# K and Q transposed by DMA from batch 2 on, and a rearranged start, in a fused local-attention and feed-forward kernel

## The chip, the cores and the metric

The kernel runs on one core of one Trainium2 chip. The metric is the time of one execution on the device in microseconds (us). Engines: TensorE (PE; its weight loads are listed as PEld), VectorE (DVE), ScalarE (ACT), GpSimd (POOL) and SyncE (SP). Each works through its own queue of instructions in order. SP and POOL also issue DMAs.

## What is computed

Eight batches of eight heads, 576 positions, head size 64. Attention is local (32 positions to each side) plus eight global positions, which see and are seen by all. Its output, 4608 rows of 512, goes through a feed-forward of 2048.

```python
scores = scale * np.matmul(q, k.transpose(0, 1, 3, 2))
mask = np.abs(pos[:, None] - pos[None, :]) <= window
mask = mask | is_global[:, None] | is_global[None, :]
scores = np.where(mask, scores, -1000000000.0)
attn = softmax(scores)                      # over the keys
x = np.matmul(attn, v)                      # to rows (batch, position) x (head, d)
h = x @ w_in
g = s * np.maximum(h, 0.0) ** 2 + b
out = g @ w_out
```

## The kernel before

**Pairs.** The 64 (batch, head) problems are taken two heads at a time: 32 pairs, four per batch. A pair has five chunks of 120 keys; the first eight of a chunk's 128 rows hold the global keys. For each chunk c, `qk` (L425) computes the scores of both heads into PSUM (tile pss, two buffers, pool ps_s), ScalarE takes the exponential (tile e), and VectorE multiplies by the mask (tile em). `pv` (L444) multiplies all five em with V (vring) and with ones (the sums), into po (one buffer). `norm_steps` (L462) are ln (s1) and exp(-ln) (s2, tile rep) on ScalarE, and the product with po into xt on VectorE; it also adds the global queries' parts up (gs), and after the fourth pair of a batch makes xg from them, which `scatter` (L498) copies into the global columns of xt on POOL, eight copies.

**K and Q.** The scores need K and Q with the head size on partitions. `load_kq` (L140) has POOL load them, cast to bf16, in a packed form (six consecutive rows on a partition, tile six, a ring of NR = 6 pairs). `trans` (L384) transposes them on TensorE, 24 small transposes per pair, into a PSUM tile pst. `trans_a` (K) and `trans_b` (Q) queue the copies out of PSUM: K by VectorE into kt (L403), Q by VectorE for one head and ScalarE for the other into qbd (L416), block-diagonal. `put_kq` (L373) adds the global columns. V is loaded as it is (`load_v`, L148, tile natv, four pairs), cast into vring (`cast_v`), and `put_v` (L366) writes the global rows.

**Globals.** For every two batches `gather` (L224) fetches the global rows of K, Q and V by indirect DMA, and the five steps of `globals_of` (L327) cast, transpose and place them; round_v and move do so for V, with 16 small matmuls each into psv and a copy to gvx (L361).

**Feed-forward.** `moe_quanta` (L508) yields 288 quanta: nine tiles of 512 rows, each with 16 psh quanta (first matrix, L523; a Relu to r on ScalarE, L530, and the square to g on VectorE, L533) and 16 pso quanta (second matrix, L538; every fourth ends with a store). `Q(n)` runs the next n, if the counter quanta allows. Sums of w_out's rows (wsum, L705) make the bias row in pairs 8 to 15; eight early output tiles are held back until it is there, and then released.

**Order.** The order on every engine is the one in which the code is written. A pair has eight slots (`run_pair`, L583): slots 0 to 4 one score chunk each, slot 6 the next pair's transposes, this pair's pv and put_v; in each slot come first its own matmuls, then extra work (ex), then the work queued in the slot before (list `later`, run as prev), then the slot's quanta. Hence the copies out of PSUM, queued in slot 6, run in slot 7. `first_pair` (L614) is the form for pairs 0 to 3, which have no feed-forward beside them: five slots, and at its end a flush of all that is queued. Between it and the loop (L669 to L697) stand pair 3's pv, pair 4's transposes, loads, scatter(0) and the weight loads. In the loop (L720), pair p first issues `load_kq(p + 4)` on POOL and `load_v(p + 3)` on SP.

Of the kernel before, what the change touches and what calls it, by code (L numbers as in the profile page):

```python
# [16 lines left out]
P = 128  # L17
B, H, S, D = 8, 8, 576, 64
NG = 8
# [16 lines left out]
NR = 6  # L36
NV = 4
NJ = 6
NP6 = S // NJ
N6 = NCH * KC // NJ  # L40
# [23 lines left out]
def kernel(  # L64
# [27 lines left out]
    stage = ctx.enter_context(tc.tile_pool(name="stage", bufs=3))  # L92
# [33 lines left out]
    six = {t: const.tile([P, NR, 2, NJ, D], BF16, name=f"six{t}", tag=f"six{t}") for t in "kq"}  # L126
    natv = const.tile([P, NV, NCH, 2, D], FP32)
# [19 lines left out]

    def load_v(eng, p):  # L148
        bi, hp = divmod(p, 4)
        for hh in range(2):  # L150
            o = v[bi, 2 * hp + hh, 0, 0].offset

            last = p == NPAIR - 1 and hh == 1
            for c, nch, n in ((0, NCH - 1, KC), (NCH - 1, 1, S - KC * (NCH - 1))) if last else (
                (0, NCH, KC),
            ):
                eng.dma_start(
                    out=natv[NG : NG + n, p % NV, c : c + nch, hh],
                    in_=bass.AP(
                        tensor=v.tensor, offset=o + c * KC * D,  # L160
                        ap=[[D, n], [KC * D, nch], [1, D]],
                    ),
                )
# [12 lines left out]
    clear(qbufs[0][0:D, 1], LQ)  # L176
    clear(qbufs[0][D:P, 0], LQ)
    clear(natv[0:NG].rearrange("p n c h d -> p (n c h d)"), NV * NCH * 2 * D)
    for t in "kq":
        nc.vector.memset(six[t][NP6:P, :, :, NJ - 1], 0.0)  # L180
    for t in gqd:
        nc.vector.memset(t[0:D, 1], 0.0)
        nc.vector.memset(t[D:P, 0], 0.0)
# [40 lines left out]
    def gather(bb):  # L224

        gfs[bb] = globp.tile([P, 3, D], FP32, tag="gf", name="gf")
        for i, t in enumerate("kqv"):
# [23 lines left out]
    load_kq(1)  # L251
    nc.vector.memset(kidx[0:NG], 100000.0)
# [34 lines left out]
    def build_masks():  # L287
        for c in range(NCH):
# [13 lines left out]
    for j in range(2):  # L302
        nc.gpsimd.dma_start(
            out=win_t[:, :, 1024 * j : 1024 * j + 1024],
            in_=w_in2[:, :, 1024 * j : 1024 * j + 1024],
        )
    greg_p = [
# [19 lines left out]
    def globals_of(bb):  # L327
# [3 lines left out]
        gvx[bb] = globp.tile([NG, 8, 2, D], BF16, tag="gvx", name="gvx")  # L331
# [22 lines left out]
        def move(i):  # L354
            ps = ps_m.tile([P, 4, 2, D], FP32, tag="moe", name="psv")
            for hp in range(4):
                for hh in range(2):
                    r0 = D * hh + 32 * i + NG * hp
                    nc.tensor.matmul(ps[:NG, hp, hh], ident[:, r0 : r0 + NG], gb[:, 2])
            later.append(  # L360
                lambda: nc.vector.tensor_copy(out=gvx[bb][:, 4 * i : 4 * i + 4], in_=ps[:NG])  # L361
            )

        return round_kq, turn, round_v, lambda: move(0), lambda: move(1)

    def put_v(eng, p):  # L366
        bb, x = divmod(p, 8)
        eng(  # L368
            out=vring[0:NG, p % NV].rearrange("g c h d -> g c (h d)"),
            in_=view(gvx[bb][:, x], [0, NCH], [1, 2 * D]),  # L370
        )

    def put_kq(p):  # L373
        bb, x = divmod(p, 8)
        nc.vector.tensor_copy(
            out=view(ktile[p][:], [P, NCH], [1, NG]),
            in_=view(gkt[bb][:, NG * x : NG * x + NG], [0, NCH], [1, NG]),
        )
# [19 lines left out]
    def trans_a(p):  # L398
        ps = trans("k", p)
        kt = ktp.tile([P, LQ], BF16, tag="kt", name="kt")  # L400
        ktile[p] = kt
# [7 lines left out]
    def trans_b(p):  # L409
# [173 lines left out]
    def run_pair(p, nq, extra):  # L583
# [3 lines left out]
        if hp == 0:  # L587
            open_batch(bi)
        for s in range(8):
# [7 lines left out]
            elif s == 5:  # L597
                if hp == 0 and bi > 1:
                    later.append(lambda: scatter(bi - 1))
            elif s == 6:  # L600
                if more:
                    trans_a(p + 1)
                    trans_b(p + 1)
                pv(p)
                pending.extend(norm_steps(p))
            if s == 6 and more:
                put_v(V if p < 7 else G, p + 1)
# [39 lines left out]
    flush()  # L647
    warm(3)
# [45 lines left out]
    load_v(nc.gpsimd, 7)  # L694
    onesf = const.tile([P, P], FP32)
# [95 lines left out]
```

## Time and profile before

| | |
|---|---|
| median of 9 runs | 397.71 us (395.76 to 397.77) |
| the profiled execution | 398.78 us |
| its span, in which the profile counts | 397.0 us |
| mean granted TensorE clock | 0.952 |
| first feed-forward matmul (psh) | 49.96 us |
| pair 8 begins | 87.35 us |
| last pair ends | about 328 us |

The page of the profile gives busy time by engine, then the span in 40 slices: each digit is the busy share in tenths, and PEclk is the TensorE clock that was granted, in tenths of full speed. A group of instructions is named by line, engine, operation and output<-input. "A <- B" in a list of waits means that A's engine stood idle until B ended. The chain of waits follows the execution back from its last instruction, at each step to what released it. Busy time of one instruction is from its start to its end; neighbours on an engine overlap, so their starts can lie closer together than their durations.

### The profile page before, as it was taken

To read this page: it belongs to the slowest core of one execution; us is meant where nothing else is said; L and a number is where in the kernel's file an instruction comes from. 1 tells how busy PE (TensorE), PEld (TensorE's weight loads), DVE (VectorE), ACT (ScalarE), POOL (GpSimd) and SP (SyncE) were. 2 spreads that over 40 slices of the span, in tenths; PEclk is the share of its full clock that TensorE was granted. 3 is DMA by queue.
4 is the path that set the end of the run, shared out by engine and by line. 5 is a ranking of instruction groups with operands and counts; after the bars stand their busy time and mean duration, and the time that the engine had idled before them with its cause. 6 is when DMAs were issued, how large, how long until landed. Compare 5 with 4: busy or idle time off the path is not lost.

```text
span 397.0 us, 9076 instructions
## 1 busy us (share of the span) xinstructions
PE 357.9 (90%) x3533; PEld 209.9 (53%) x3533; DVE 262.2 (66%) x648; ACT 216.2 (54%) x416; POOL 128.5 (32%) x224
## 2 busy tenths in 40 slices
PE   6766398899899979899989998999999999999996
PEld 2343244455555556456755775567656654554442
DVE  5764557677987798778877777687667763432431
ACT  5665558744684467446764676357745761630710
POOL 7753186145760560229600900383004001000000
PEclk8775579999999999999999999999999999999999
DMA  5999389835981290059534840575021002001002
GB/s 96 185 209 201 67 149 187 170 57 99 225 155 50 29 202 2 26 128 186 128 99 125 165 74 2 115 151 87 2 85 54 2 0 82 29 22 64 21 26 79
DMA packets 56558, 38.07 MB, mean 96 GB/s; under 512 B 34792, under 2 KB 49128, under 8 KB 56516
## 3 DMA queue, kind: packets, MB, share of 16 engines
q0 software_dynamic: 18784, 20.07, 30.0%
q1 hardware_dynamic: 37732, 17.43, 17.3%
q8 instruction: 27, 0.44, 0.5%
q14 instruction: 15, 0.12, 0.1%
HBM read 41.68 MB, written 9.44 MB: 129 GB/s over the span
## 4 chain that ended last, share of the span: by engine, by line
PE 63%; DVE 18%; ACT 13%; issue 3%; DMA 2%; ACTq 0%; DVEq 0%; POOLq 0%
PE pso L538 30%; PE psh L523 17%; PE po L453 6%; PE pss L427 5%; ACT r L530 4%; DVE g L533 4%; DVE em L434 3%; PE pst L392 3%; ACT qbd L416 3%; DVE xt L490 3%; ACT e L431 2%; DVE qbd L416 2%; DVE kt L403 2%; DVE wsum L705 2%; DMA sixk<-in_k_dram 2%
## 5 line engine op out<-in xcount | busy, mean ns | idle before, releaser
L523 PE MATMUL psh<-xt,win_t 128*128 128x512 bf16 (+7 forms) x1024 | 141.7, 289 | 0.0
L538 PE MATMUL pso<-wout_t,g 128*128 128x512 bf16 x576 | 137.1, 379 | 1.8 <-DVE gvx L361 1.8
L530 ACT ACTIVATE r<-psh 128x512 bf16<-128x512 f32 x144 | 87.9, 627 | 66.6 <-PE psh L523 64.1
L523 PEld LDWEIGHTS <-win_t 128*128 128x128 bf16 x1024 | 85.6, 98 | 48.8 <-issue 6.1
L431 ACT ACTIVATE e<-pss 128x384 bf16<-128x384 f32 (+1 forms) x160 | 76.5, 483 | 36.5 <-PE pss L427 32.1
L533 DVE TENSOR_TENSOR g<-r 128x512 bf16<-128x512 bf16 x144 | 64.0, 448 | 43.7 <-ACT r L530 41.4
L538 PEld LDWEIGHTS <-g 128*128 128x128 bf16 x576 | 54.5, 98 | 65.3 <-issue 5.1
L434 DVE TENSOR_TENSOR em<-e,mask 128x384 bf16<-128x384 bf16 (+1 forms) x160 | 62.3, 392 | 21.3 <-ACT e L431 20.8
L427 PE MATMUL pss<-qbd,kt 128*128 128x384 bf16 (+1 forms) x160 | 51.3, 330 | 20.8 <-ACT qbd L416 16.7
L501 POOL COPY xt<-xg 128x4 bf16 x64 | 14.4, 225 | 124.5 <-DVE xt L490 120.9
L416 ACT COPY qbd<-pst 64x600 bf16<-64x600 bf16 x32 | 20.9, 653 | 54.5 <-DVE qbd L416 54.3
L552 DVE SCALAR_TENSOR_TENSOR osb<-pso,s_bc,bias_row 128x512 f32<-128x512 f32 x28 | 20.9, 747 | 37.4 <-PE pso L538 37.4
L368 POOL COPY vring<-gvx 8x640 bf16<-8x640 bf16 x24 | 18.4, 769 | 55.3 <-DVE gvx L361 54.0
L427 PEld LDWEIGHTS <-kt 128*128 128x128 bf16 x160 | 15.4, 99 | 30.2 <-DVE qbd L379 11.2
L490 DVE TENSOR_TENSOR xt<-po,rep 128x600 bf16<-128x600 f32 x32 | 24.9, 779 | 4.7 <-ACT rep L488 4.3
L453 PE MATMUL po<-em,vring 128*64 128x160 bf16 (+3 forms) x448 | 21.8, 231 | 6.7 <-DVE xt L490 6.4
L403 DVE COPY kt<-pst 128x600 bf16<-128x600 bf16 x32 | 24.8, 774 | 4.1 <-PE pst L392 4.1
L484 ACT ACTIVATE ln<-po 128x640 f32<-128x640 f32 x32 | 22.6, 706 | 5.1 <-PE po L453 5.1
L416 DVE COPY qbd<-pst 64x600 bf16<-64x600 bf16 x32 | 24.5, 765 | 0.7 <-PE pst L392 0.7
L488 ACT ACTIVATE rep<-ln 128x640 f32<-128x640 f32 x32 | 24.3, 759 | 0.1
L453 PEld LDWEIGHTS <-vring 128*64 128x64 bf16 x448 | 18.3, 117 | 9.9 <-DVE xt L490 5.8
L143 POOL DMA_DIRECT2D sixk<-in_k_dram x32 | 21.3, 664 | 6.8 <-issue 5.9
(81 smaller groups left out, 269.5 us busy)
## 6 DMA issues: line engine op xcount, KB each, us to landing
natv<-in_v_dram SPq DMA_DIRECT2D x51, 150.0 KB, 3.9
out_dram<-osb SPq DMA_DIRECT2D x28, 256.0 KB, 2.1
sixk<-in_k_dram POOLq DMA_DIRECT2D x32, 144.0 KB
sixq<-in_q_dram POOLq DMA_DIRECT2D x32, 144.0 KB
wst<-in_moe_w_out_dram POOLq DMA_DIRECT2D x8, 512.0 KB
win_t<-in_moe_w_in_dram POOLq DMA_DIRECT2D x2, 1024.0 KB
wout_t<-in_moe_w_out_dram POOLq DMA_DIRECT2D x4, 512.0 KB
out_dram<-osbh SPq DMA_DIRECT2D x8, 256.0 KB
```

What stands on the lines that cost most here:

```text
L403: lambda: nc.vector.tensor_copy(out=view(kt[:, NG:], [P, NCH], [NJ, KC // NJ], [1, NJ]), in_=view(ps[:], [KC // NJ, NCH], [1, KC // NJ], [ ...
L416: eng(out=view(qbufs[p % 3][r, hh], [P, NCH], [HB + NG, 2], [NJ, n], [1, NJ]), in_=view(ps[r], [2 * n, NCH], [n, 2], [1, n], [NP6, NJ]),)
L427: nc.tensor.matmul(ps[:], ktile[p][:, P * c : P * c + P], qbufs[p % 3][:, :, LO[c] : HI[c]])
L431: nc.scalar.activation(e[:], ps[:], AF.Exp, scale=SCALE)
L434: later.append(lambda: nc.vector.tensor_mul(em[:], e[:], masks[c]))
L453: nc.tensor.matmul(po[D * hh : D * hh + D, a : a + n], onesb[:] if part else vring[:, p % NV, c, hh], emt[(p, c)][:, hh, x : x + n], start ...
L488: nc.scalar.activation(rep[:], ln[:], AF.Exp, scale=-1.0)
L490: lambda: nc.vector.tensor_tensor(out=xt[:, hp].rearrange("p (c a j) -> p c a j", c=NCH, a=2), in0=halves(po[:, 0:LQ]), in1=halves(rep[:]) ...
L523: nc.tensor.matmul(psh[:, d0 : d0 + n], win_t[:, a, f * P : f * P + P], xts[bi][:, a, x0 : x0 + n], start=(a == 0 and j == 0), stop=(a == ...
L530: nc.scalar.activation(r[:], psh[:], AF.Relu)
L533: later.append(lambda g=g, r=r: nc.vector.tensor_mul(g[:], r[:], r[:]))
L538: nc.tensor.matmul(pso[:], gl[f][:, u * P : u * P + P], wout_t[:, f], start=(f == 0), stop=(f == 15),)
```

## The change

Three things. **From batch 2 on (pairs 8 to 31)** K and Q are loaded in their natural layout, in fp32, by SP (`load_nat`, with V), four pairs ahead. ScalarE casts them into natb (`round_nat`) in slots 5 and 7 of pair p-2. One transposing DMA of SP (`turn_nat`), 128 x 1280 elements of bf16 between SBUF tensors, follows in slot 7. In slot 5 of pair p-1 `place_nat` uses K where it landed, copies Q's halves into qbd with two VectorE copies, and calls put_kq. The global rows of V for batches 2 to 7 come by eight POOL loads into gvall, so the gathers fetch only K and Q there, and put_v stays on VectorE. **In the first pairs** the copies out of PSUM go into the slot of their transposes (list now), put_v and cast_v stand in other slots, the flush at the end is gone, V's global steps of batch 0 come after pair 0, and the masks are built in two parts. **Pair 4** runs its score slots as a fifth first pair, and only its slots 5 to 7 in run_pair, with 0, 1 and 2 quanta where all its slots had 6. Pairs 8 to 31 have one quantum per slot as before, so the three fall to the end. All weight loads, gvall and gather(1) stand ahead of scatter(0) in POOL's order.

```diff
-NR = 6
+NR = 5
 NV = 4
+NSIX = 8
+KT0 = 16
+QT0 = KT0 + NCH * P
...
+    nat = {t: const.tile([P, NV, NCH, 2, D], FP32, name=f"nat{t}", tag=f"nat{t}") for t in "kq"}
+    natb = [const.tile([P, 2, NCH * P], BF16, name=f"natb{i}", tag=f"natb{i}") for i in range(2)]
...
+    def load_nat(eng, t, p):
+        bi, hp = divmod(p, 4)
+        dst = natv if t == "v" else nat[t]
+        parts = ((0, 0, HB), (HB, HB, HB)) if t == "q" else ((NG if t == "v" else 0, 0, KC),)
+        for hh in range(2):
+            o = src[t][bi, 2 * hp + hh, 0, 0].offset
+            for r, a, n in parts:
+                runs = [(0, NCH, n)]
+                if p == NPAIR - 1 and hh == 1:
+                    runs = [(0, NCH - 1, n), (NCH - 1, 1, min(n, S - KC * (NCH - 1) - a))]
+                for c, nch, m in runs:
+                    eng.dma_start(
+                        out=dst[r : r + m, p % NV, c : c + nch, hh],
+                        in_=bass.AP(
+                            tensor=src[t].tensor, offset=o + (c * KC + a) * D,
+                            ap=[[D, m], [KC * D, nch], [1, D]],
+                        ),
+                    )
     def load_v(eng, p):
-        bi, hp = divmod(p, 4)
+        load_nat(eng, "v", p)
+    kqt = {}
+    def round_nat(i, t, p):
+        nc.scalar.copy(
+            out=natb[p % 2][0:KC, i].rearrange("p (c h d) -> p c h d", c=NCH, h=2),
+            in_=nat[t][0:KC, p % NV],
+        )
+    def turn_nat(p):
+        kqt[p] = kqp.tile([P, QT0 + NCH * P], BF16, tag="kqt", name="kqt")
+        nc.sync.dma_start_transpose(
+            out=kqt[p][:, KT0:].rearrange("p (c x) -> p c x", x=P),
+            in_=natb[p % 2][:].rearrange("p t x -> p (t x)"),
+        )
+    def place_nat(p):
+        ktile[p] = kqt[p][:, KT0 - NG : KT0 - NG + LQ]
         for hh in range(2):
-            o = v[bi, 2 * hp + hh, 0, 0].offset
-            last = p == NPAIR - 1 and hh == 1
-            for c, nch, n in ((0, NCH - 1, KC), (NCH - 1, 1, S - KC * (NCH - 1))) if last else (
-                (0, NCH, KC),
-            ):
-                eng.dma_start(
-                    out=natv[NG : NG + n, p % NV, c : c + nch, hh],
-                    in_=bass.AP(
-                        tensor=v.tensor, offset=o + c * KC * D,
-                        ap=[[D, n], [KC * D, nch], [1, D]],
-                    ),
-                )
+            r = slice(D * hh, D * hh + D)
+            nc.vector.tensor_copy(
+                out=view(qbufs[p % 3][r, hh], [P, NCH], [HB + NG, 2], [1, HB]),
+                in_=view(kqt[p][r, QT0:], [P, NCH], [HB, 2], [1, HB]),
+            )
+        put_kq(p)
...
-    def gather(bb):
+    def gather(bb, ts="kq"):
...
     gather(0)
     load_kq(1)
+    gather(0, "v")
...
             in_=w_in2[:, :, 1024 * j : 1024 * j + 1024],
         )
+        if j == 0:
+            load_kq(4)
...
+        if bb:
+            return round_kq, turn
         return round_kq, turn, round_v, lambda: move(0), lambda: move(1)
...
-        bb, x = divmod(p, 8)
+        g = gvx[0][:, 2 * D * p :] if p < 8 else gvall[:, 2 * D * (p - 8) :]
         eng(
             out=vring[0:NG, p % NV].rearrange("g c h d -> g c (h d)"),
-            in_=view(gvx[bb][:, x], [0, NCH], [1, 2 * D]),
...
-    def trans_a(p):
+    def trans_a(p, later=later):
...
-    def trans_b(p):
+    def trans_b(p, later=later):
...
-        if hp == 0:
+        if hp == 0 and p > 4:
             open_batch(bi)
-        for s in range(8):
+        for s in range(8) if p > 4 else range(NCH, 8):
             prev, later[:] = list(later), []
             if s < NCH:
                 qk(p, s)
                 if s == 2 and more:
                     cast_v(A if p < 7 else G, p + 1)
             elif s == 5:
-                if hp == 0 and bi > 1:
+                if hp == 0:
                     later.append(lambda: scatter(bi - 1))
+                if p == 4:
+                    cast_v(A, 5)
             elif s == 6:
-                if more:
+                if p + 1 < NSIX:
                     trans_a(p + 1)
                     trans_b(p + 1)
                 pv(p)
                 pending.extend(norm_steps(p))
             if s == 6 and more:
-                put_v(V if p < 7 else G, p + 1)
+                put_v(V, p + 1)
             for f in extra.get(s, ()):
                 f()
             for f in prev:
     def first_pair(p):
-        if p == 0:
-            open_batch(0)
+        if p % 4 == 0:
+            open_batch(p // 4)
         for s in range(NCH):
             prev, later[:] = list(later), []
+            now = []
             qk(p, s)
             if s in (1, 2):
-                if p < 3:
-                    (trans_a, trans_b)[s - 1](p + 1)
+                if p < 4:
+                    (trans_a, trans_b)[s - 1](p + 1, now)
                 if p:
                     pv(p - 1, (s - 1,))
                     if s == 2:
                         pending.extend(norm_steps(p - 1))
             elif s > 2:
                 step()
-                if s == 3 and p < 3:
+                if s == 4 and p < 4:
                     cast_v(A, p + 1)
-            for f in prev:
+            for f in prev + now:
                 f()
-            if s == 4 and p < 3:
-                put_v(V, p + 1)
-        flush()
+            if s == 3 and p:
+                put_v(V, p)
...
     warm(12)
     trans_a(0)
     flush()
+    build_masks((0, 1))
     warm(3)
     trans_b(0)
     warm(8)
     flush()
     steps0 = globals_of(0)
-    build_masks()
     steps0[0]()
     steps0[1]()
-    warm(4)
+    warm(2)
     flush()
     put_kq(0)
+    build_masks((2, 3, 4))
     cast_v(A, 0)
-    for t in qbufs[1:]:
-        clear(t[0:D, 1], LQ)
-        clear(t[D:P, 0], LQ)
+    first_pair(0)
     for f in steps0[2:]:
         f()
     flush()
     put_v(V, 0)
-    for p in range(4):
+    load_v(nc.gpsimd, 4)
+    load_kq(5)
+    for p in (1, 2, 3, 4):
         first_pair(p)
-    pv(3)
-    pending.extend(norm_steps(3))
+        if p == 1:
+            load_v(nc.gpsimd, 5)
     for i in (1, 2, 3):
         rows_of(i)
-    for p in (4, 5):
-        load_kq(p)
-        load_v(nc.gpsimd, p)
     load_w_out(0)
     load_w_out(1)
     load_kq(6)
-    step()
-    trans_a(4)
-    flush()
-    step()
-    cast_v(A, 4)
-    trans_b(4)
-    flush()
-    put_v(V, 4)
-    scatter(0)
     nc.sync.dma_start(out=s_bc[:], in_=_bcast_dram(moe_s[:], P))
     nc.sync.dma_start(out=b_bc[:], in_=_bcast_dram(moe_b[:], P))
     load_v(nc.gpsimd, 6)
...
     load_w_out(3)
     load_kq(7)
     load_v(nc.gpsimd, 7)
+    gvall = const.tile([NG, (B - 2) * H * D], BF16)
+    for i in range(NG):
+        nc.gpsimd.dma_start(
+            out=gvall[i : i + 1].rearrange("o (b h d) -> o b h d", b=B - 2, h=H),
+            in_=v[2:, :, ds(greg_p[i], 1), :].rearrange("b h o d -> o b h d"),
+        )
     onesf = const.tile([P, P], FP32)
     nc.vector.memset(onesf[:], 1.0)
     quanta[0] = 32
...
         bi, hp = divmod(p, 4)
         nq = [1] * 8
         if bi == 1:
-            nq = [0, 1, 1, 1, 0, 1, 1, 1] if hp else [0, 0, 1, 1, 1, 1, 1, 1]
+            nq = [0, 1, 1, 1, 0, 1, 1, 1] if hp else [0, 0, 0, 0, 0, 0, 1, 2]
         elif hp == 0:
             quanta[0] += 32
         if p + 4 < NPAIR:
-            load_kq(p + 4)
-        if p >= 5 and p + 3 < NPAIR:
-            load_v(nc.sync, p + 3)
+            for t in "kqv":
+                load_nat(nc.sync, t, p + 4)
         if p % 8 == 4 and p + 4 < NPAIR:
             gather((p + 4) // 8)
         ex = {}
-        if p % 8 == 7 and p + 1 < NPAIR:
-            for s, f in enumerate(globals_of((p + 1) // 8)):
-                ex.setdefault(s, []).append(f)
+        def at(s, f, *a):
+            ex.setdefault(s, []).append(lambda: f(*a))
+        if p >= 6 and p + 2 < NPAIR:
+            at(5, round_nat, 0, "k", p + 2)
+            at(7, round_nat, 1, "q", p + 2)
+            at(7, turn_nat, p + 2)
+        if p % 8 > 4 and p + 3 < NPAIR:
+            if p % 8 == 5:
+                steps = globals_of((p + 4) // 8)
+                at(7, steps[0])
+            elif p % 8 == 6:
+                at(1, steps[1])
+        if p >= 7 and p + 1 < NPAIR:
+            at(5, place_nat, p + 1)
         if 8 <= p < 15:
             for s in (4, 7):
                 if adds:
-                    ex.setdefault(s, []).append(adds.pop(0))
+                    at(s, adds.pop(0))
         if 7 <= p < 15:
             adds.extend(wpiece(p - 7))
         if p == 15:
-            ex.setdefault(2, []).append(lambda: [f() for f in adds] and adds.clear())
-            ex[2].append(bias)
+            for f in adds:
+                at(2, f)
+            at(2, bias)
         if p > 15 and held_rows:
-            ex.setdefault(4, []).append(release)
-            ex.setdefault(7, []).append(release)
+            at(4, release)
         run_pair(p, nq, ex)
     flush()
     while pending:
```

More of the change, by code (lines that the diff above doesn't have):

```diff
@@ L91 @@
     mop = ctx.enter_context(tc.tile_pool(name="mop", bufs=3))
-    stage = ctx.enter_context(tc.tile_pool(name="stage", bufs=3))
+    stage = ctx.enter_context(tc.tile_pool(name="stage", bufs=2))
+    kqp = ctx.enter_context(tc.tile_pool(name="kqp", bufs=2))
     globp = ctx.enter_context(tc.tile_pool(name="globp", bufs=2))
@@ L174, in clear @@
         nc.scalar.copy(out=ap, in_=view(zero[0 : ap.shape[0]], [0, n]))
-    clear(qbufs[0][0:D, 1], LQ)
-    clear(qbufs[0][D:P, 0], LQ)
+    for t in qbufs[:2]:
+        clear(t[0:D, 1], LQ)
+        clear(t[D:P, 0], LQ)
     clear(natv[0:NG].rearrange("p n c h d -> p (n c h d)"), NV * NCH * 2 * D)
+    clear(qbufs[2][0:D, 1], LQ)
+    clear(qbufs[2][D:P, 0], LQ)
     for t in "kq":
         nc.vector.memset(six[t][NP6:P, :, :, NJ - 1], 0.0)
+    for t in natb:
+        nc.vector.memset(t[96:P], 0.0)
     for t in gqd:
@@ L222 @@
     gfs = {}
-    def gather(bb):
-        gfs[bb] = globp.tile([P, 3, D], FP32, tag="gf", name="gf")
-        for i, t in enumerate("kqv"):
+    def gather(bb, ts="kq"):
+        if bb not in gfs:
+            gfs[bb] = globp.tile([P, 3, D], FP32, tag="gf", name="gf")
+        for t in ts:
+            i = "kqv".index(t)
             nc.gpsimd.indirect_dma_start(
@@ L285, with build_masks @@
     masks = []
-    def build_masks():
-        for c in range(NCH):
+    def build_masks(cs):
+        for c in cs:
             m = const.tile([P, W[c]], BF16, name=f"mask{c}", tag=f"mask{c}")
@@ L330, in globals_of @@
         gkt[bb] = globp.tile([P, D], BF16, tag="gkt", name="gkt")
-        gvx[bb] = globp.tile([NG, 8, 2, D], BF16, tag="gvx", name="gvx")
+        if bb == 0:
+            gvx[0] = const.tile([NG, 16 * D], BF16, name="gvx", tag="gvx")
         def round_kq():
@@ L360, in move @@
             later.append(
-                lambda: nc.vector.tensor_copy(out=gvx[bb][:, 4 * i : 4 * i + 4], in_=ps[:NG])
-            )
+                lambda: nc.vector.tensor_copy(
+                    out=gvx[bb][:, 512 * i : 512 * i + 512],
+                    in_=ps[:NG].rearrange("g a h d -> g (a h d)"),
+                )
+            )
+        if bb:
+            return round_kq, turn
         return round_kq, turn, round_v, lambda: move(0), lambda: move(1)
     def put_v(eng, p):
-        bb, x = divmod(p, 8)
+        g = gvx[0][:, 2 * D * p :] if p < 8 else gvall[:, 2 * D * (p - 8) :]
         eng(
             out=vring[0:NG, p % NV].rearrange("g c h d -> g c (h d)"),
-            in_=view(gvx[bb][:, x], [0, NCH], [1, 2 * D]),
+            in_=view(g, [0, NCH], [1, 2 * D]),
         )
@@ L375, in put_kq @@
         nc.vector.tensor_copy(
-            out=view(ktile[p][:], [P, NCH], [1, NG]),
+            out=view(ktile[p], [P, NCH], [1, NG]),
             in_=view(gkt[bb][:, NG * x : NG * x + NG], [0, NCH], [1, NG]),
@@ L396, in trans @@
         return ps
-    def trans_a(p):
+    def trans_a(p, later=later):
         ps = trans("k", p)
         kt = ktp.tile([P, LQ], BF16, tag="kt", name="kt")
-        ktile[p] = kt
+        ktile[p] = kt[:]
         later.append(
@@ L694 @@
     load_v(nc.gpsimd, 7)
+    gvall = const.tile([NG, (B - 2) * H * D], BF16)
[3 more added lines that the diff above has]
+            in_=v[2:, :, ds(greg_p[i], 1), :].rearrange("b h o d -> o b h d"),
+        )
     onesf = const.tile([P, P], FP32)
```

## The prediction, made before the changed kernel ran

> **What bounds the kernel now.** I read the page first (busy shares, slices), then TensorE's waits by stage, the chain of waits, then single pairs in the timeline.
>
> ```profile
> PE 357.9 (90%) x3533; PEld 209.9 (53%) x3533; DVE 262.2 (66%) x648; ACT 216.2 (54%) x416; POOL 128.5 (32%) x224
> ...
> PE   6766398899899979899989998999999999999996
> ...
> PEclk8775579999999999999999999999999999999999
> ```
>
> TensorE is the busiest engine, and full from about the eighth slice (80 us) on, at the whole granted clock. Before that it has holes, and its clock falls (0.50 from 30 to 55 us). I cut the span in three: a head up to 87.35 us (pairs 0 to 7), the stage of pairs 8 to 31 (87.35 to 328.0), and a tail of feed-forward alone. The middle stage (length, then busy us and instructions of PE, PEld, DVE, ACT, POOL, then clock, DMA share, GB/s), and TensorE's waits in it (total, times, longest):
>
> ```profile
> 87.35:328.00 240.65, 227.57 (x2507) 144.41 (x2507) 182.57 (x430) 142.98 (x287) 81.46 (x144) 1.00 0.44 92
> ```
> ```profile
> PE pss L427 <- ACT qbd L416: 8.5, 12, 1.8
> PE po L453 <- DVE xt L490: 2.2, 5, 1.0
> PE pso L538 <- DVE gvx L361: 1.8, 2, 0.9
> ```
>
> TensorE works 227.57 of 240.65 us. Of the 13.1 idle us, 8.5 are one wait: a pair's first scores wait until its transposed Q has been copied out of PSUM. So this stage gets shorter by what leaves TensorE and by that wait, and by little else. The chain shows one pair (start, us, what):
>
> ```profile
> 306.26 1.75 PE psh L523 x16
> 308.01 0.64 PE pst L392 x24
> 308.65 0.85 PE po L453 x28
> 309.50 0.99 PE psh L523 x8
> 310.49 0.02 issue
> 310.51 0.60 ACT r L530
> 311.11 0.02 issue
> 311.13 0.66 ACT qbd L416
> ```
>
> Here are both: 24 transposes (0.64 us) on the path, and later the copy of Q, behind a Relu on ScalarE, that ends the idle time.
>
> **Part 1: the transposes leave TensorE for pairs 8 to 31.** 24 pairs x 0.64 us = -15.4. The wait for the Q copy, -8.5: the copy goes, and the new copies stand at slot 5 of the pair before. V's rows of the global keys now come by eight loads once, so 32 small matmuls of the stage (1.6 us busy) and the wait on gvx (1.8) go: -3.4, of which I take 3.0. Sum **-26.9**.
>
> **Part 2: what comes in, on VectorE.** Removed per pair: two PSUM copies (775 and 765 ns). Added: two copies of 64x600 between SBUF tensors (not in this trace; the nearest row, an 8x640 copy of vring, starts the next instruction after 0.37 us; bounds 0.17, a 128x80 copy, and 0.77, the PSUM copy), and the vring copy moved over from GpSimd (0.37). Volume is about even (1.4 us out, 1.1 in), but the place matters. This is VectorE around the end of a pair that began at 311.84:
>
> ```profile
> 317.08 0.78 DVE L490 TENSOR_TENSOR xt<-po,rep 128x600 bf16<-128x600 f32 x1 [0.26 <-ACT rep L488]
> 317.78 0.41 DVE L533 TENSOR_TENSOR g<-r 128x512 bf16<-128x512 bf16 x1
> 318.11 0.32 DVE L434 TENSOR_TENSOR em<-e,mask 128x320 bf16<-128x320 bf16 x1
> ```
>
> The last em ends 6.55 us into the pair. TensorE reaches the pv matmuls at 6.64 now (318.48), at 6.09 without transposes, and needs that em 0.33 us later (11 of 14 matmuls of the first half come before it). The new copies stand ahead of this em in VectorE's queue: 2 x 0.37 and the two small ones that put the global columns (0.18) make 0.92, so em ends at about 7.35 and TensorE stands still for 0.9 us. That holds where the pair computes psh (ScalarE is late with rep). In pso pairs, rep and xt come earlier, and with 21 instead of 24 quanta done at pair 8 the output stores leave slot 4; there I get 0 to 0.2. So 12 x 0.9 = **+10.8**; bounds 0 and 24 x 1.3 = 31.
>
> **Part 3: ScalarE.** Out: 653 ns per pair (Q's second half). In: two casts of 120x640 (the same cast of V: 733 ns). In a psh pair its instructions start 0.5 us (r), 0.36 (e), 0.58 (ln), 0.62 (rep) apart: 4.0 + 1.8 + 1.2, and with 2 x 0.61 it is 8.2 of some 9.6 us (8.7 + 0.9). It stays just below TensorE: 0. If psh pairs had two casts too many, it would be 12 x 0.7 = 8.
>
> **Part 4: SP and the DMA queues.** K and Q change from two casting loads on POOL (0.64 us each to issue) to six plain ones on SP beside V's two: 8 issues of 0.47 to 0.68 us, 3.8 to 5.4 us per pair; with the transposing DMA and up to two stores (0.37) SP is occupied 5 to 7 of the 8.7 us that a pair would take (pv to pv now 299.33 to 308.65, less 0.64). Loads are issued four pairs ahead, so their own delay is covered. In bytes: V's 150 KB move at 182 to 256 GB/s, about 0.75 us each, so 885 KB a pair are 4.4 us of DMA time. This fits too: 0.
>
> What is not covered is the transposing DMA. It is issued at the end of pair p-2, behind the second cast on ScalarE (which ends where the Q copy ends now, at the end of the pair), and VectorE's copies at slot 5 of pair p-1 read it: some 5.3 us later behind a psh pair, up to 8 behind a pso pair, where ScalarE is early. The trace has no such DMA. Its bounds from landings: 2.0 us (a store of 256 KB) and 10 (V's slowest load, 9.0, and another 0.75 for twice the bytes, rounded up). I take V's median of 3.9 plus 170 KB more at about 200 GB/s (0.85): 4.8 us, just inside. If it is late, nothing hides it: VectorE stands still in order, with the em behind it, and TensorE waits for pv, 24 us of the total per us of lateness.
>
> No run here shows a transposing DMA, and the Trainium skill says two things. "VectorE: DVE Perf Modes", section "The three transpose paths", gives 1309 ns for a 128x128 block by DMA against 390 ns on TensorE; ten blocks one after another would be an estimated 13 us, which is far too late. "Advanced Engine Details and Errata", section "X-Bar Transpose (TRN2)", has these transposes as fast as regular DMAs, 350 to 400 GB/s, an estimated 0.9 us for 328 KB. By the one the kernel loses over 100 us, by the other it ends at my forecast; I go by the V loads.
>
> **Part 5: the head.** In pairs 1 to 3 the chain runs xt, pv, ln, the V cast, the Q copy, e, rep, xt: 28.95 to 36.63, 7.68 us. With the copy in its own slot and the cast after rep, two ScalarE pieces (0.61 + 0.65, with gaps) leave it: about 6.3. Pair 4 without the gap between 44.3 and 48.7 has its scores by some 45 us. But the first feed-forward needs scatter(0), and POOL comes to it late. Now it waits for xg (idle 12.46) and copies from 47.38 to 49.45. Afterwards, from 34.92 on, it must first issue load_v 6 and 7 (3.7), w_out 2 and 3 (1.55), load_kq(7) (1.4), eight gvall rows (not in the trace; between 0.64, a K load, and 1.33, an indirect one; 0.85 x 8 = 6.8) and gather(1) (2.8): 51.2, and 2.07 for the scatter, 53.3. Three quanta at half and full clock (1.71 + 1.71 + 0.86) lead to 57.6, where pair 5 starts with 3 quanta done; now it starts at 60.24 with 6. The missing 3 x 0.863 = 2.6 come back in the tail: 60.2. Sum **0**; bounds -6.5 (POOL not late) and +6 (it waits on outstanding DMAs, as the 3.7 and 2.6 us waits behind win_t and wout_t show).
>
> **The sum.** The profiled execution took 398.78 us, 1.78 around its span; the median is 397.71, 1.07 less. 398.78 - 26.9 + 10.8 + 0 = 382.7, on the median's scale 381.6: **382 us**. With Parts 2 and 5 at their likelier bounds, 372 to 390.
>
> **Rivals.**
> (a) *The transposed K and Q land late* (slower). For it: unknown length, only 5.3 us in half the pairs, SP's queue in front. Against: V's landings. The gain of 16.1 us is used up by 0.67 us of lateness per pair, so from a latency near 6 us on it is slower. At 7.5 us, 2.2 late: 382 + 53 = 435; at 10 us, 382 + 24 x 4.7 = 495.
> (b) *The copies' place eats the gain.* If all 24 pairs wait 0.9 us for em, or ScalarE's casts delay psh pairs by 0.7: +8 to +11, and with the head's +6: 390 to 398.
> (c) *The idle time stays.* If the wait for Q is only replaced by that for another evacuation (xt, 2.2 now), the 8.5 stays: 390. It lies inside (b).
>
> **How the numbers follow.** Forecast 0.50 (372 to 390), (b) with (c) 0.14 (390 to 398.5), (a) 0.36 (above 398.5). About 0.2% is what a measurement of this kernel can tell from no change; 0.04 of (b) lies within it. Faster 0.60, same 0.04, slower 0.36. The range leaves out 0.03 below 372 and, above 434, about half of (a): 372 to 434. The forecast's own range is 372 to 390.
>
> **What would show it.** Right: no L392 groups after pair 7, none of TensorE's waits on qbd in the stage, pairs of 8.7 (pso) to 9.6 us (psh), a new wait of TensorE's pv or its weight load on em of up to 1 us, the first psh near 53 us. Wrong: VectorE's new copies idle before themselves, released by the transposing DMA; or psh pairs where TensorE waits on ScalarE's e behind a cast.

## The result, and the profile after

| | before | after |
|---|---|---|
| median, us | 397.64 (31 runs) | 400.64 (10 runs, 399.72 to 402.46) |
| ratio | | 1.0083, 95% interval 1.0068 to 1.0099 |
| profiled execution / its span, us | 398.78 / 397.0 | 400.22 / 398.4 |
| mean granted TensorE clock | 0.952 | 0.930 |
| first psh matmul, us | 49.96 | 64.50 |
| pair 7's pv, second half begins (A) | 85.09 | 94.97 |
| pair 31's pv, second half begins (B) | 328.31 | 326.86 |

The kernel became slower by 0.8%. The second half of pv (the 14 matmuls that multiply with onesb, a tile of ones; one group per pair in the timeline) is a mark that both traces have for every pair, and it cuts the span: up to A, +9.9 us; from A to B, which is 24 pairs, 243.2 to 231.9, -11.3; after B, 68.7 to 71.5, +2.8. The sum is +1.4, the difference of the spans. So the stage did get shorter, and the head and the tail gave more than that back.

The page of the kernel after: busy times, then three rows of slices (TensorE, its clock, DMA).

```profile
PE 345.7 (87%) x2907; PEld 198.8 (50%) x2907; DVE 241.6 (61%) x665; ACT 227.3 (57%) x440; POOL 78.7 (20%) x157
...
PE   6687605889998999799989999999999999999995
...
PEclk9855555999999999999999999999999999999999
DMA  5999998109979998899879987997755102001002
```

TensorE has 12.2 us less work than before (345.7 against 357.9), and the time is longer. The sixth digit of its row, 0, is the slice from about 50 to 60 us: TensorE stands still in it, at half the clock, while the DMA engines are full. Its waits over the whole span (total, times, longest), and then those of the 24 pairs alone, after the line of that stretch (columns as in the prediction):

```profile
PE psh L579 <- POOL xt L557: 16.0, 1, 16.0
PE po L509 <- DVE em L490: 13.1, 22, 0.9
PE po L509 <- DVE xt L546: 3.7, 7, 1.1
```
```profile
97.26:326.50 229.24, 214.12 (x1921) 133.07 (x1921) 163.01 (x447) 153.34 (x308) 35.38 (x80) 1.00 0.86 156
```
```profile
PE po L509 <- DVE em L490: 12.5, 21, 0.9
PE psb L764 <- DVE wsum L758: 1.4, 1, 1.4
PE po L509 <- DVE xt L546: 0.7, 2, 0.4
```

There are two stalls: one of 16.0 us, once, in the head (L557 is the scatter's copy on POOL), and 21 small ones in the stage. The wait for the copy of Q, 8.5 us before, is gone. The first stall is read from POOL's queue (start, duration, what; in brackets the idle time before it and what ended it):

```profile
46.37 1.83 POOL L168 DMA_DIRECT2D natv<-in_v_dram  x2 [0.54 <-ACT vring L206]
48.20 0.56 POOL L744 DMA_DIRECT2D gvall<-in_v_dram  x1
...
51.76 0.52 POOL L744 DMA_DIRECT2D gvall<-in_v_dram  x1 [2.16 <-DMA wout_t<-in_moe_w_out_dram]
55.15 0.52 POOL L744 DMA_DIRECT2D gvall<-in_v_dram  x1 [2.87 <-DMA wout_t<-in_moe_w_out_dram]
...
59.23 0.52 POOL L744 DMA_DIRECT2D gvall<-in_v_dram  x1 [0.44 <-DMA natv<-in_v_dram]
60.10 1.00 POOL L275 DMA_INDIRECT gf<-in_k_dram,grow  x1 [0.35 <-issue]
61.41 0.99 POOL L275 DMA_INDIRECT gf<-in_q_dram,grow  x1 [0.30 <-issue]
62.38 2.07 POOL L557 COPY xt<-xg 128x4 bf16 x8
```

Eight loads of 6 KB, 0.52 us each to issue (4.2 together), take from 48.20 to 59.75, because POOL stood still ahead of seven of them until some earlier DMA had landed. That DMA was each time the one that POOL had issued eight places before. In all twelve traces POOL's DMAs use eight semaphores (counters that tell of a landing) in strict turn, and a DMA waits for the last one with the same semaphore: the third gvall load could start only at 51.76, when w_out 2, issued at 40.03, had landed. Behind the eight loads come gather(1) and only then the scatter, for which all of TensorE waits. Pair 4's pv had been done since 48.5. In the kernel before, POOL came to the scatter in time, stood idle for xg, and issued the loads behind it:

```profile
47.38 2.07 POOL L501 COPY xt<-xg 128x4 bf16 x8 [12.46 <-DVE xt L490]
49.82 1.84 POOL L157 DMA_DIRECT2D natv<-in_v_dram  x2 [0.37 <-ACT e L431]
```

The second stall, in VectorE's queue at the end of a psh pair:

```profile
121.51 0.78 DVE L546 TENSOR_TENSOR xt<-po,rep 128x600 bf16<-128x600 f32 x1
122.20 0.42 DVE L589 TENSOR_TENSOR g<-r 128x512 bf16<-128x512 bf16 x1
122.53 0.69 DVE L199 COPY qbd<-kqt 64x600 bf16<-64x600 bf16 x2
123.23 0.18 DVE L431 COPY kqt<-gkt 128x40 bf16<-128x40 bf16 x1
123.32 0.18 DVE L435 COPY qbd<-gqd 128x80 bf16<-128x80 bf16 x1
123.41 0.32 DVE L490 TENSOR_TENSOR em<-e,mask 128x320 bf16<-128x320 bf16 x1
```

The last em starts behind place_nat's four copies (L199 to L435) and ends at 123.73. On TensorE, pv's matmuls that need it start at 123.78 after 0.93 us of idle time.

One of e10's six executions, the profiled one, was slow, 386.22 us against 374.59 to 380.06, and e10's time and ratio below are those of the other five.

### The profile page after: what moved, and what is told of

It reads as the page before. It is cut to its first block, busy times and chain, and to the rows that moved or that the text cites. A ratio compares the mean times of both kernels' runs of the same rounds, so it can differ in the third digit from the quotient of the medians.

```text
span 398.4 us, 8035 instructions
## 1 busy us (share of the span) xinstructions
PE 345.7 (87%) x2907; PEld 198.8 (50%) x2907; DVE 241.6 (61%) x665; ACT 227.3 (57%) x440; POOL 78.7 (20%) x157
## 4 chain that ended last, share of the span: by engine, by line
PE 47%; DVE 24%; ACT 17%; issue 6%; DMA 4%; POOL 1%; ACTq 0%; POOLq 0%; DVEq 0%
PE pso L594 22%; PE psh L579 13%; PE po L509 7%; ACT r L586 7%; DVE xt L546 5%; DVE em L490 5%; ACT e L487 4%; DVE g L589 4%; DVE qbd L199 3%; PE pss L483 3%; DMA natv<-in_v_dram 3%; ACT rep L544 2%; ACT ln L540 2%; DMA sixk<-in_k_dram 2%; DVE wsum L758 1%
## 5 line engine op out<-in xcount | busy, mean ns | idle before, releaser
L490 DVE TENSOR_TENSOR em<-e,mask 128x384 bf16<-128x384 bf16 (+1 forms) x160 | 56.1, 351 | 22.4 <-ACT e L487 21.9
L557 POOL COPY xt<-xg 128x4 bf16 x64 | 14.4, 225 | 165.7 <-DVE xt L546 162.3
L509 PE MATMUL po<-em,vring 128*64 128x160 bf16 (+3 forms) x448 | 25.8, 237 | 17.3 <-DVE em L490 13.1
L483 PE MATMUL pss<-qbd,kqt 128*128 128x384 bf16 (+1 forms) x120 | 37.8, 315 | 0.0
L509 PEld LDWEIGHTS <-vring 128*64 128x64 bf16 x448 | 20.0, 117 | 29.1 <-issue 20.2
L544 ACT ACTIVATE rep<-ln 128x640 f32<-128x640 f32 x32 | 24.4, 763 | 0.0
L206 POOL CAST vring<-natv 128x640 bf16<-128x640 f32 x24 | 17.9, 764 | 31.0 <-DMA natv<-in_v_dram 16.3
L509 PE MATMUL po<-em,onesb 128*64 128x160 bf16 (+2 forms) x448 | 21.6, 234 | 0.0
L483 PE MATMUL pss<-qbd,kt 128*128 128x384 bf16 (+1 forms) x40 | 14.2, 398 | 5.2 <-ACT e L487 3.2
L182 ACT CAST natb<-natk 120x640 bf16<-120x640 f32 x24 | 18.2, 759 | 0.0
L182 ACT CAST natb<-natq 120x640 bf16<-120x640 f32 x24 | 17.7, 739 | 0.0
L509 PEld LDWEIGHTS <-onesb 128*64 128x64 bf16 x448 | 16.8, 120 | 0.3 <-issue 0.3
```

The source lines that it names most:

```text
L182: nc.scalar.copy(out=natb[p % 2][0:KC, i].rearrange("p (c h d) -> p c h d", c=NCH, h=2), in_=nat[t][0:KC, p % NV],)
L483: nc.tensor.matmul(ps[:], ktile[p][:, P * c : P * c + P], qbufs[p % 3][:, :, LO[c] : HI[c]])
L490: later.append(lambda: nc.vector.tensor_mul(em[:], e[:], masks[c]))
L509: nc.tensor.matmul(po[D * hh : D * hh + D, a : a + n], onesb[:] if part else vring[:, p % NV, c, hh], emt[(p, c)][:, hh, x : x + n], start ...
L544: nc.scalar.activation(rep[:], ln[:], AF.Exp, scale=-1.0)
```

## The experiments

My theory after the result: (A) the head is lost in POOL's queue, where scatter(0) stands behind the gvall loads and whatever they wait for; (C) the stage's missing part is place_nat's place in VectorE's queue. The rivals: (B) the head is lost to SP's early loads of K, Q and V, which fill the DMA engines; and, for the stage, that the transposing DMA lands late.

**e1_gvall_behind.** The gvall loads and gather(1) go behind scatter(0).

```diff
-        if p % 8 == 4 and p + 4 < NPAIR:
+        if p % 8 == 4 and 4 < p and p + 4 < NPAIR:
...
         run_pair(p, nq, ex)
+        if p == 4:
+            load_gvall()
+            gather(1)
```

> The changed kernel with one move: the eight gvall loads and gather(1) are issued by POOL after pair 4's last slots, so behind scatter(0). Theory A (POOL's order: in the changed kernel scatter(0) stood behind ten loads that waited for outstanding DMAs, first psh at 64.5 us): POOL is through with load_v(7) at 48.2, so scatter ends near 50.5, the first psh stands at 50 to 52, and 12 to 14 us go: 387 to 389 us. Theory B (the DMA engines are saturated until 65 us by the early loads of K and Q, the order hardly matters): the stall comes back at the next transfer that is late (w_out, V of pairs 6 and 7), less than 6 us go: 395 to 400 us.

389.82 us, ratio 0.9838 (0.9796 to 0.9880). The first psh of e1:

```profile
50.39 3.52 PE L579 MATMUL psh<-xt,win_t 128*128 128x512 bf16 x12 [0.37 <-POOL xt L557]
```

The wait of 16.0 us is 0.37. But 3.65 us came back later, at pair 6's scores: VectorE's cast of the gathered globals (L385) now waited 3.18 us for gather(1), the last in POOL's queue, and the scores waited for what VectorE does behind it. That is A, 0.8 us above its range of 387 to 389.

**e2_loads_behind.** As e1, and load_v(6) and (7), w_out 2 and 3 and load_kq(7) also behind scatter(0), in front of the gvall loads.

```diff
+        if p == 4:
+            load_v(nc.gpsimd, 6)
+            load_w_out(2)
+            load_w_out(3)
+            load_kq(7)
+            load_v(nc.gpsimd, 7)
+            load_gvall()
+            gather(1)
```

> As the run before, and load_v(6), w_out 2 and 3, load_kq(7) and load_v(7) stand behind scatter(0) too, as in the kernel before. Theory A: scatter starts when xg is ready (about 46 us), the first psh at about 48.5, where TensorE has ended pair 4's pv: 16 us go against the changed kernel, 383 to 386 us. Theory B: pair 5 to 7 wait for V, K or w_out instead, 393 us or more.

397.32 us, 1.0024 (0.9997 to 1.0050): the expected gain did not come. The first psh started at 48.52. Then, on VectorE and on TensorE:

```profile
71.41 0.23 DVE L385 CAST gb<-gf 128x128 bf16<-128x128 f32 x1 [11.98 <-DMA gf<-in_q_dram,grow]
```
```profile
73.75 0.75 PE L483 MATMUL pss<-qbd,kt 128*128 128x320 bf16 x2 [12.42 <-ACT qbd L472]
```

I had put gather(1) behind still more loads, so it was issued at 67.48, and the stall moved from pair 5 to pair 6, with 12.42 of its 16.0 us. The miss supports A in one thing: POOL's queue in these 20 us is longer than the time there is, and what stands last in it is what the kernel waits for.

**e3_sp_held.** POOL's order as in the change; SP's early loads are held until scatter(0) is done, by a small copy out of xts[0] that stands ahead of them in SP's queue.

```diff
+    scr = const.tile([1, 600], BF16)
...
-        if p + 4 < NPAIR:
+        if p + 4 < NPAIR and p > 4:
             for t in "kqv":
                 load_nat(nc.sync, t, p + 4)
...
         run_pair(p, nq, ex)
+        if p == 4:
+            nc.sync.dma_start(out=scr[0:1], in_=xts[0][0:1, 0, 0:600])
+            for t in "kqv":
+                load_nat(nc.sync, t, 8)
```

> The changed kernel with POOL's order as it is, but SP holds the loads of K, Q and V for pair 8 and later back until scatter(0) is done (a small copy of its result stands ahead of them in SP's queue). Theory A: POOL still has to issue all its loads first; with some 2.4 MB less in the DMA queues (about 11 us at 210 GB/s) its waits for outstanding DMAs shrink, and the first psh comes at 53 to 58 us: 389 to 394 us. Theory B (SP's loads alone made the stall): first psh at 50 or earlier and 14 us or more go, 386 us or less. If neither counts: 400 us.

395.59 us, 0.9972 (0.9944 to 1.0000). In e3 the first psh stands here:

```profile
58.18 4.53 PE L579 MATMUL psh<-xt,win_t 128*128 128x512 bf16 x12 [10.12 <-POOL xt L557]
```

So B has a share: without SP's loads in the way, POOL's waits end some 6 us earlier (64.50 to 58.18). The other 10 us are POOL's own queue. The time gained, 5.1 us, is less than A had expected (389 to 394 us).

**e4_place_slot6.** The change with place_nat one slot later, behind the last em.

```diff
-            at(5, place_nat, p + 1)
+            at(6, place_nat, p + 1)
```

> The changed kernel with one move: Q's copies and the global columns (place_nat) in slot 6 instead of slot 5, behind the pair's last em in VectorE's queue. Theory C (their place ahead of em makes TensorE's pv wait, 12.5 us in 21 waits): these waits go, and 8 to 12 us with them, 389 to 393 us. Rival D: VectorE is late anyway, the next pair's first scores wait for the copies instead, as they waited for the Q copy in the kernel before (8.5 us): 398 to 401 us.

383.97 us, 0.9682 (0.9644 to 0.9720), 16.7 us less than the change as it is. VectorE at the end of a pair in e4:

```profile
117.80 0.32 DVE L490 TENSOR_TENSOR em<-e,mask 128x320 bf16<-128x320 bf16 x1
118.37 0.47 DVE L424 COPY vring<-gvall 8x640 bf16<-8x640 bf16 x1
118.77 0.68 DVE L199 COPY qbd<-kqt 64x600 bf16<-64x600 bf16 x2
```

The em comes first, TensorE's wait on em is in no row of e4 any more, and A to B takes 217.4 us, against 231.9 in the change. The wait of the first psh is still 14.0. C holds, with more than I had expected of it (389 to 393 us). (The profiled executions differ by 17.9 us in span: 14.5 in the stage, 3.4 up to A.)

**e5_order.** A better order on POOL, with place_nat left in slot 5: gather(1) stays ahead of scatter(0), the loads for pairs 6 and 7 go behind it, the gvall loads behind pair 5.

```diff
         run_pair(p, nq, ex)
+        if p == 4:
+            load_v(nc.gpsimd, 6)
+            load_w_out(2)
+            load_w_out(3)
+            load_kq(7)
+            load_v(nc.gpsimd, 7)
+        if p == 5:
+            load_gvall()
```

> The changed kernel with POOL's order mended in another way: load_v(6), w_out 2 and 3, load_kq(7) and load_v(7) after pair 4 (behind scatter(0)), gvall after pair 5, gather(1) left ahead of scatter(0). In the run before with all of it behind scatter(0), the first psh came at 48.5 us but pair 6 waited 12.4 us for VectorE's cast of gather(1), which stood last in POOL's queue. Theory A (POOL's order is the whole of the head's loss): first psh at 48 to 49 us, no long wait in pairs 5 to 7, pair 8's pv about 16 us earlier than in the changed kernel: 383 to 386 us. Theory B (the DMA engines are full in any order): another transfer is late by 5 us or more, V of pair 6 or 7, or gvall before pair 8: 390 us or more.

390.29 us (387.18 to 391.62), 0.9843 (0.9804 to 0.9883). The head is mended: first psh at 50.92, A at 81.46 instead of 94.97, no long wait in pairs 5 to 7. The median lies 4 us above what I had expected, and in B's range, though no transfer is late as B has it; the profiled execution is the fastest of the four, and what the others lose isn't shown. A to B, 232.5, is that of the change: the order on POOL doesn't touch the stage.

**e6_order_place6.** e4's and e5's edits together.

> The same order of POOL together with place_nat in slot 6. If the head's loss and the wait of pv for em are separate costs, the gains add: 16 + 16.7 us off the changed kernel, 367 to 371 us. If the earlier head meets transposing DMAs that land late (more DMA traffic per us), place_nat waits for them and only part adds: 372 to 380 us.

371.31 us, 0.9350 (0.9315 to 0.9385), the fastest kernel here, 6.5% below the kernel before. Its 24 pairs (83.00 to 298.58), as a stretch:

```profile
83.00:298.58 215.58, 210.80 (x1921) 132.09 (x1937) 163.95 (x447) 153.20 (x308) 37.49 (x80) 1.00 0.95 167
```

The same 1921 matmuls as after the change, and 4.8 us of idle time instead of 15.1. Most pairs now take 8.74 to 9.2 us.

**e7_dma_alone.** The kernel before with the transposing DMA for pairs 8 to 31 and the buffers that it needs (NR = 5, two buffers in the pool stage instead of three): neither the new start nor the gvall loads, K and Q four pairs ahead on SP, place_nat in slot 5.

```diff
         if p + 4 < NPAIR:
-            load_kq(p + 4)
+            for t in "kq":
+                load_nat(nc.sync, t, p + 4)
...
+        if p >= 6 and p + 2 < NPAIR:
+            ex.setdefault(5, []).append(lambda p=p: round_nat(0, "k", p + 2))
+            ex.setdefault(7, []).append(lambda p=p: round_nat(1, "q", p + 2))
+            ex.setdefault(7, []).append(lambda p=p: turn_nat(p + 2))
+        if p >= 7 and p + 1 < NPAIR:
+            ex.setdefault(5, []).append(lambda p=p: place_nat(p + 1))
```

> The kernel before with the transposing DMA alone: K and Q of pairs 8 to 31 by load_nat, round_nat, turn_nat and place_nat (slot 5), as in the changed kernel; first pairs, pair 4, the V globals by gather and put_v on GpSimd as before. Theory A (the stage of pairs 8 to 31 gains some 11 us, the head alone loses): pair 8 begins at 87 to 90 us, the stage takes about 230 us instead of 240.7, 385 to 389 us. Rival (the loads of K and Q on SP disturb the head in this order too): pair 8 begins later than 93 us, 392 us or more.

398.54 us, 1.0028 (1.0003 to 1.0054). I had expected a gain here; the transposing DMA by itself gave none. The cause is again em, here in all 24 pairs (TensorE's waits in e7):

```profile
PE po L507 <- DVE em L488: 19.8, 24, 1.9
```

With 24 quanta done at pair 8, as before, an output step (osb, 0.74 us) stands in the pso pairs between xt and the new copies; with the change's 21 it comes a slot earlier. So the place costs more here than in the change, and A to B (239.5) gains only 3.8 of 243.2. A itself comes 2.9 us later than in the kernel before (87.97 against 85.09); 1.9 of that is the longest of these waits, in pair 7, just ahead of A.

**e9_dma_alone_place6.** e7 with place_nat in slot 6.

> The kernel before with the transposing DMA alone, place_nat in slot 6 instead of slot 5. The same with slot 5 came to 398.5 us, with TensorE's pv waiting 19.8 us for em. Theory C (place_nat ahead of em takes back nearly all that the transposes free): pairs of 8.7 to 9.2 us instead of 9.5 to 10.1, 24 x 0.9 = 22 us, 375 to 380 us. Rival D (the stage is limited elsewhere without the new start, by POOL's copies or the score wait): 388 us or more.

374.29 us, 0.9445 (0.9412 to 0.9478). One digit of e7, the slot, is worth 24 us. TensorE's waits on em in e9:

```profile
PE po L507 <- DVE em L488: 0.3, 1, 0.3
```

And e9 against e6 tells what the rest of the change is worth once nothing hides it. A to B: 220.5 in e9, 217.1 in e6, -3.4, the size that I had counted for V's global rows before I took 3.0; no run takes them alone. A: 82.76 and 81.52, but e6 has three quanta fewer done by then, which cost 2.6 in the tail. So the new start, with pair 4's pv at 48.2 instead of 54.8, comes to -1.2 + 2.6 = +1.4 in these two executions. In them the pv of pair 0 already stands 2.7 us apart (21.73 in e9, 24.45 in e6), so a gain or loss of this size isn't shown. In both kernels the first psh starts near 50 us (48.5 and 51.8). In e6 it waits 1.76 us for the scatter, which stands behind gather(1) on POOL; in e9 the scatter is through at 48.0, and TensorE waits 3.52 us for VectorE ahead of pair 4's first scores.

**e8_place_slot1.** A measurement of the disputed latency: the change with place_nat in slot 1, so early that VectorE must wait for the transposing DMA in nearly every pair.

```diff
-            at(5, place_nat, p + 1)
+            at(1, place_nat, p + 1)
```

> A measurement: the changed kernel with place_nat in slot 1 of the pair before, some 1 to 2 us after the transposing DMA is issued, so that VectorE stands still until it lands and its wait shows the time from issue to landing. By my estimate from V's loads it is 4.8 us; by ten blocks at 1.3 us, an estimate from the Trainium skill's page VectorE: DVE Perf Modes, it would be 13. The kernel should be slower than the changed one by 24 times what is then missing, 2 to 4 us a pair: 440 to 490 us, or over 600 with 13.

430.94 us (one execution), less than the 440 to 490 that I had expected. VectorE's waits in e8:

```profile
DVE qbd L199 <- DMA kqt<-natb: 48.8, 22, 4.1
```

From the start of SP's issue to the copy's start it takes 3.4 to 5.6 us, about 4 in the middle. (TensorE's wait on em, 13.1 us in the change, is in no row of e8; its wait on xt grows from 3.7 to 31.1.)

**e10_order_place6_sp_held.** e6 with e3's hold on SP.

> The kernel with POOL's order mended and place_nat in slot 6 (371.3 us), and SP's loads for pairs 8 and later held back until scatter(0) is done. If the early loads of K and Q still delay the head there (first psh 51.8 us against 48.5 with everything behind scatter(0), pair 6 waits 1 us), 2 to 4 us go: 367 to 370 us. If they then come late for pair 8 or crowd the transposing DMAs, 372 us or more.

376.08 us, 0.9484 (0.9453 to 0.9514), 5 us more than e6: what I had expected did not come, the hold is a loss. In its profiled execution VectorE's waits have a row that e6 has only with 0.2 us:

```profile
DVE qbd L199 <- DMA kqt<-natb: 13.7, 3, 5.9
```

Held loads crowd into the time in which the first transposing DMAs run, and three of those land late. That is rival (a) of the prediction. Whether the same waits make the 5 us of the other executions isn't shown.

## Why the prediction was wrong, step by step

**The step that failed is Part 5, the head.** I took 0, with a first psh at 53.3, and kept +6 for waits on outstanding DMAs. Head and tail came to +12.7 (9.9 and 2.8), with the first psh at 64.50. The issues were counted rightly and even too dearly (gvall 0.52 each, not 0.85). What failed was the assumption that POOL issues them one after another: each has to wait until the load eight places before it has landed. I had it reach the scatter at 51.2; it did at 62.38. Of these 11.2 us, 3.3 were lost before load_v(6) (38.22, not 34.92; a 4.06 us wait for w_in's load stands there), 3.3 more before the gvall loads (48.20, not 41.6; three waits of 0.98, 1.93 and 0.54 around load_kq(7)), and 4.7 in them: 11.55 us instead of 6.8, of which 7.3 were seven waits for earlier loads of w_out, K, Q and V to land. SP's first loads of K, Q and V slowed these landings (e3: about 6 us). I had seen two such waits of 3.7 and 2.6 us in the trace of before and made a bound of them, where so many more DMAs, at a time when the DMA engines are full, called for a term of the sum. Both waits (ahead of 30.40 and 62.74) already go eight places back, so the trace of before held the rule by which to work the term out. The tail's part, 2.6 for three quanta, was right (2.8).

**Part 2 had the right place and too small a size.** Forecast 0.9 us in 12 psh pairs, +10.8. Measured: up to 0.93 in psh pairs as forecast, but 0.45 to 0.49 in most pso pairs too, where I had 0 to 0.2. There VectorE is late for another reason, the output steps, for example osb (0.74) and the held rows' bias (0.68) just ahead of em and xt. With e4 as the reference the place costs 231.9 - 217.4 = 14.5. The copies themselves were close: 0.69 for the two, forecast 0.74. (The sum has a slip: 6.55 and 0.92 make 7.47, not 7.35, and a wait of 1.05 instead of 0.93. So that its 0.9 was met is in part luck.)

**Part 1 was nearly right.** Forecast -26.9 without the place. A to B in e4 is 217.4, -25.8 against 243.2. The wait on Q (8.5) and gvx went. The transposes were worth less than their busy time: a pso pair that waited for nothing took 9.26 us before and takes 8.74 in e4 and e9, so 0.52 each and, if the psh pairs lose as much, 12.5 in all, not 15.4. With 8.5 and 3.4 that makes 24.4 of the 25.8; what the rest is isn't shown. The 0.64 us that the chain shows from one group's start to the next one's is not what removing the group brings.

**Part 3, ScalarE: 0.** Right: TensorE has no row of waits on e in the stage. The casts took 739 and 759 ns, V's had taken 733, and the next instruction starts 0.61 us after a cast of K, as forecast.

**Part 4, the landing: right.** 4.8 us forecast, 3.4 to 5.6 measured (e8), and in the changed kernel no VectorE wait on it at all. The DMA engines' share in the stage went from 0.44 to 0.86, which stayed hidden. Of the two sections of the Trainium skill that I weighed, the per-block figure of "VectorE: DVE Perf Modes", "The three transpose paths", would have made an estimated 13 us of ten blocks; e8 speaks against adding blocks up. "X-Bar Transpose (TRN2)" in "Advanced Engine Details and Errata" has the throughput of regular DMAs, an estimated 0.9 us; e8's 4 us are nearer to V's landings than to either.

**The rivals.** Not (a), which I had made the main one. It is (b) with both of its halves, the place and the head's bound, each larger than priced: 400.6 against 390 to 398.5. (c) did not come: TensorE's wait on xt fell from 2.2 to 0.7. So the forecast's sign turned on +12.7 where I had 0; the 3.7 us more for the place alone would have left the kernel faster.

## What to carry to other kernels

An instruction that is added to a queue must be costed at its place: ask which instruction behind it somebody waits for. Here one slot for four short copies was worth 17 to 24 us, more than the 12.5 us of all the transposes that they replace. A queue that issues DMAs is not costed by its issue times when the DMA engines are full: look in the trace which earlier DMA an issue waits for, and when that one lands. Put first in the queue what computes for others. And a wait in the trace of before, on a resource that the change loads further, is a term of the sum and no bound.

## What the runs showed of the hardware

A load of 6 KB can hold POOL's queue for up to 2.87 us, until the larger load eight places before it has landed. The wait is for a semaphore that the program's own instructions name, and no run has more than eight of them, so what more would bring isn't shown. SP's issues stretch as well: in the full stretch, two loads of K took 6.13 us from 41.33 on and four of Q 9.41 from 47.51 on. The transposing DMA (128x1280 bf16, between SBUF tensors) takes SP longer to issue where the DMA engines are full: in e4, four issues at a DMA share of 0.10 to 0.39 took 1.33 to 1.36 us, and four at 0.81 to 1.51 took 2.05 to 3.00. Its landing can grow too. In e4 from 132 to 146 us (the stretch's line ends with the DMA share, 1.26, and 208 GB/s), SP's queue and then VectorE's:

```profile
137.44 2.34 SPq L189 DMA_TRANSPOSE kqt<-natb  x1
```
```profile
145.58 0.70 DVE L199 COPY qbd<-kqt 64x600 bf16<-64x600 bf16 x2 [0.46 <-DMA kqt<-natb]
```

2.34 us to issue and 8.1 from there to the copy, which waited 0.46 for it. In slot 6 of that pair the DMA was just late; it is the only wait on it in e4.

And VectorE's em became faster on average. The groups of the mask multiply from 100 to 300 us, first before, then after (xcount | busy, mean ns | idle):

```profile
L434 DVE TENSOR_TENSOR em<-e,mask 128x384 bf16<-128x384 bf16 x59 | 27.3, 465 | 8.9 <-ACT e L431 8.7
```
```profile
L490 DVE TENSOR_TENSOR em<-e,mask 128x384 bf16<-128x384 bf16 x62 | 22.0, 354 | 7.3 <-ACT e L487 7.3
```

The same instruction takes 465 and 354 ns. POOL was busy for 71.2 us of these 200 before, and for 34.2 after; in e7 and e9, at 48.6 and 51.3, em takes 369 and 379. The trace of before tells more than the means. Of its 59, 47 took 343 to 360 ns, as after the change, and 12 took 828 to 1340, more than double. All 12 have an instruction of POOL beside them, 11 of them one of its copies or casts; of the 47, only 6 have one: gathers, issues, and one cast that started after the em. One of the 12, POOL and VectorE:

```profile
138.53 0.94 POOL L368 COPY vring<-gvx 8x640 bf16<-8x640 bf16 x1
138.86 0.83 DVE L434 TENSOR_TENSOR em<-e,mask 128x384 bf16<-128x384 bf16 x1
```

So em is stretched where POOL works beside it. No run varied POOL's work alone, and which of its instructions it takes isn't shown.
